# Attention features, Mish layer and top-1 experts on one core: last activation products and logits placed earlier, register loads placed later

## The chip, the cores and the metric

The kernel runs on one core of a Trainium2 chip. The metric is the device time of one execution in microseconds, the median of several runs. The engines are TensorE (PE; its weight loads are listed apart as PEld), VectorE (DVE), ScalarE (ACT), GpSimd (POOL) and SyncE (SP, which here only issues transfers).

## What is computed

Three layers in a row: random-feature attention, a dense layer with Mish as its activation, and a mixture of 8 experts of which each token takes one.

```python
# attention: phi is exp of (projection - norm - max); per head
num = q_p @ (k_p.T @ v);  den = q_p @ sum(k_p) + 1e-6;  x = num / den
# dense layer, 1152 tokens, 512 -> 2048 -> 512
h = x @ w_in
g = h * tanh(log1p(exp(h)))
y = g @ w_out
# experts: logits, softmax, the best expert of a token, its place, capacity
logits = y @ w_gate
out[i] = gate_w[i] * (relu(y[i] @ w1[e]) @ w2[e])      # where the place is under the capacity
```

## The kernel before

Matrix products that need float32 are done as three products of rounded halves (`mm3`, L69 to L74): a tile is split into a rounded high half (`round_hi`, L52, on ScalarE, GpSimd or VectorE) and a remainder (`take_lo`, L62, on VectorE or GpSimd).

**Attention**, up to about 76 us. It goes over 8 pairs of heads. For each pair the transposed keys and queries (`kqf`) are loaded, split (`split`, with the engines named by `halves`, L226) and projected (`pj`); VectorE takes the negated maximum (`nm`, L259), ScalarE forms `e` (L266, L269), and TensorE forms the sums `kvp`, transposes (`qt`) and the quotient's parts (`den`, `num`). The order in which the engines get these instructions isn't fixed by hand. For pair 1 the two pieces of `kqf` (512 and 768 columns) are rounded on ScalarE, and GpSimd takes their remainders.

**The h stage**, to about 182 us, from here on in the order written (`tc.manual_schedule()`). It goes over 16 chunks `j` of 128 hidden units, each with three column blocks `c` of 384 tokens: `h` by `hmm`, the copy to `g` by `hout`, and beside them the conversion of the next weights (`conv64` through `advance(wi)`, `advance(wo1)`: generators that issue one VectorE instruction at each step), the pieces of the activation (`mish`: sigmoid, logarithm, tanh on ScalarE, then the product `tp` on VectorE, L500), and the gate weights. These fold `w_out` into `w_gate`: `wturn(j)` transposes a chunk of `w_out` into `woT` on VectorE (L465), `wgate(b)` multiplies four such chunks (`wu`, L471) after chunks 4, 8 and 12. The logits (`lg`, L506) are then made from `g` itself, four chunks at a time.

**y of group 1**, from about 185 to 218 us. The tokens are in four groups of 288. The loop over 16 chunks multiplies `g` by `w_out` (`ymm`, 12 products a chunk). `g_split(j + 2)` rounds `g` two chunks ahead, in three buffers; `wo_split` splits the `w_out` chunks. Into the same loop are written the last activation products (`mish("tp", ...)`), the last logits behind chunk 7, and the routing: `route0` (maximum and place), `route1` (counts), `gates`, and `route2`, a generator that finds the most used expert of group 1 and the group and expert that come second, and loads these numbers into registers (`eA`, `g1`, `eB`; L762 to L764) of SP, VectorE and, for `g1`, ScalarE. `advance(*[chain] * pace)` takes `pace` steps of it a chunk.

**Group 2 and the experts**, to the end. Group 2's `y` goes like group 1's, with its columns chosen by the register `g1`, while the first expert's weights are loaded by SP (`expert_load`, by `eA`). Then the two experts' layers run, each followed by its output: the copies to `yo` (the last at L932), transposes, weighting by `wA` or `wB`, and the transfer to memory. If any token is left over, a slow general path follows; it isn't taken here.

The loop of group 1, in its middle part before the change:

```python
e = "pool" if j < 6 else "act"
if 0 < j < NJ - 2:
    g_split(j + 2, all0, e, "dve")
if 0 < j < NJ - 6:
    wo_split(j + 6, e, "dve")
if j in (4, 5, 6):
    mish("tp", j + 9)
```

Of the kernel before, what the change touches and what calls it, by code (L numbers as in the profile page):

```python
# [33 lines left out]
def performer_mish_moe(  # L34
# [123 lines left out]
    def advance(*gens):  # L158

        for x in gens:  # L160
            next(x, None)

    def finish(*gens):

        for x in gens:
            for _ in x:
                pass
# [18 lines left out]
    with ExitStack() as c2:  # L186
# [38 lines left out]

        def halves(p):  # L226

            return (("act", "dve"),) * 3 if p == 0 else (("act", "pool"),) * 2 if p == 1 else (("pool", "pool"),) * 5

        def split(p):  # L230
            d = st[p]
# [215 lines left out]
    with tc.manual_schedule():  # L447
# [77 lines left out]
        def wo_split(j, ehi, elo):  # L525
            wo_hi(j, ehi)
            wo_lo(j, elo)
# [13 lines left out]
        def ymm(ps, j):  # L541

            t, w = ghl.pop(j), chunk["wo", j]
            for d in range(KT):
                s = slice(d * 128, d * 128 + 128)
                mm3(ps[d][:, :GT], w[0][:, s], w[1][:, s], t[:, 0, :], t[:, 1, :], j == 0, j == NJ - 1)
# [38 lines left out]
        for j in range(NJ):  # L585
            if j + 4 < NJ:
                fetch("wi", j + 4)
            for i in (j + 2,) if j < 12 else (14, 15) if j == 12 else ():
                fetch("wo", i)
            if j == 6:  # L590
                nc.sync.dma_start(
                    out=out.rearrange("(p t) d -> p (t d)", p=128).rearrange("p (c f) -> p c f", f=128),
                    in_=zero[:, None, :].to_broadcast([128, NT * DM // 128 // 128, 128]),
                )
            if j in (9, 13):
                logits((j - 9) // 4)
            wi = convert("wi", j + 3) if j + 3 < NJ else iter(())
            wo1 = convert("wo", j + 1) if j < 14 else iter(())
            wo2 = convert("wo", 15) if j == 13 else iter(())
            for c in range(3):  # L600
                if (j, c) not in h_early:
                    hout(j, c, hmm(j, c))
                if j == 14 and c == 0:
                    wo_hi(0, "pool")
                    wo_hi(1, "pool")
                if j == 15 and c == 0:
                    wo_hi(2, "pool")
                    for i in range(3):
                        g_hi(i, all0, "pool")
                if c == 0:  # L610
                    advance(wi, wo1, late, wi)
                    late = wi
                    if j == 15:
                        wturn(j)
                if c == 1:
                    if j in (4, 8, 12):
                        gates_of[0] = wgate(j // 4 - 1)
                        next(gates_of[0])
                    advance(wi, wi, wo1, wo2)
                    if j in (5, 9, 13):  # L620
                        advance(gates_of[0])
                if c == 2:
                    advance(wo1, wo2)
                    if j in (4, 8, 12, 5, 9, 13):
                        advance(gates_of[0])
                    if j < 15:
                        wturn(j)
                    advance(wo2)
                for x in at.get(3 * j + c, ()):
                    x()  # L630
                if 3 * j + c in (44, 45, 46):
                    wo_lo(3 * j + c - 44, "dve")
                if j == 15 and c > 0:
                    for i in range(3):
                        if (i > 0) == (c == 2):
                            g_lo(i, all0, "dve")
                if j == 14 and c == 2:
                    fpool.release()
                    y3 = tc.alloc_tile_pool(name="y3", bufs=3, side="right", reuse_waits="tile")
                    whA = tc.alloc_tile_pool(name="whA", bufs=7, side="right", reuse_waits="tile")  # L640
# [89 lines left out]
        def route2():  # L730
# [28 lines left out]
            R["ri"] = ri  # L759
            ET = mybir.EngineType  # L760
            why = "an index computed from constants and a maximum's place"
            R["eA"] = nc.values_load(ri[0:1, 0:1], engines=[ET.SP, ET.DVE], min_val=0, max_val=E - 1, skip_runtime_bounds_check_because=why)  # L762
            R["g1"] = nc.values_load(ri[0:1, 1:2], engines=[ET.SP, ET.DVE, ET.Activation], min_val=0, max_val=G - 2, skip_runtime_bounds_check_because=why)
            R["eB"] = nc.values_load(ri[0:1, 2:3], engines=[ET.SP, ET.DVE], min_val=0, max_val=E - 1, skip_runtime_bounds_check_because=why)  # L764
            wA, wB = small("wA", [TT, 3]), small("wB", [TT, 3])
            V.tensor_copy(out=wA, in_=R["wt"][:, 0:3, ds(R["eA"], 1)].rearrange("p t e -> p (t e)"))
            yield
            V.tensor_copy(out=wB, in_=R["wt"][:, ds(R["g1"] * 3 + 3, 3), ds(R["eB"], 1)].rearrange("p t e -> p (t e)"))
            yield
            R["wA"], R["wB"] = wA, wB  # L770
            rem = small("rem", [1, 1])
# [55 lines left out]
        for j in range(NJ):  # L827

            if j == 0:
                for i in range(3, 7):  # L830
                    wo_lo(i, "dve")
            e = "pool" if j < 6 else "act"
            if 0 < j < NJ - 2:
                g_split(j + 2, all0, e, "dve")
            if 0 < j < NJ - 6:
                wo_split(j + 6, e, "dve")
            if j in (4, 5, 6):
                mish("tp", j + 9)
            advance(*[chain] * pace)
            ymm(ps0, j)  # L840
            if j in (2, 3):
                advance(gates_of[0])
            if j == 7:
                logits(3)
                lgs = h3.tile([128, NT], F32, name="lgs", tag="em2")
                S.copy(out=lgs[:, 0:384], in_=lg[0])
                V.tensor_copy(out=lgs[:, 384:768], in_=lg[1])
                S.copy(out=lgs[:, 768:1152], in_=lg[2])
            if j == 8:
                finish(route0(lgs))  # L850
            if j == 11:
                route1()
            if j == 12:
                chain, pace = route2(), 7
                advance(chain)
            if j == 13:
                finish(gates())
        advance(*[chain] * 40)
        colB = ds(R["g1"] * GT + GT, GT)
        g_split(0, colB, "act", "dve")  # L860
        g_split(1, colB, "act", "dve")
# [4 lines left out]
        for j in range(NJ):  # L866
            if j + 2 < NJ:
                g_split(j + 2, colB, "act", "dve")
            ymm(ps1, j)
            expert_load(R["eA"], 0, j)  # L870
            if j >= 4:
                expert_split(0, j - 4, "act", "dve")
# [56 lines left out]
                (S.copy if d % 2 else V.tensor_copy)(out=yo[:, d, :], in_=py[d][:, :GT])  # L929
        for t in range(3):  # L930
            c = slice(t * TT, t * TT + TT)
            (V.tensor_copy if t == 1 else S.copy)(out=yo[:, 3, c], in_=py[3][:, c])  # L932
        for t in range(3):
            turn(pt[t], yo, t, 3)
        send(3, slice(384, 512))
# [122 lines left out]
```

## Time and profile before

| | us |
|---|---|
| median of 3 runs | 306.43 (306.09 to 306.73) |
| profiled execution, its own time | 306.35 |
| its span in the profile | 304.6 |
| TensorE busy | 294.3 (97%) |
| VectorE busy | 215.8 (71%) |
| ScalarE busy | 186.5 (61%) |
| GpSimd busy | 76.1 (25%) |

The span is the time between the first and the last instruction of the profile; the execution's own time has what lies around it. Busy time on TensorE counts an instruction from its start to a modelled end, and successive ones overlap. Times in the rows below are from the span's start. A bracket at the end of a timeline's line gives how long the engine sat idle before it and what it waited for.

### The profile page before, as it was taken

How to read it: one execution, taken by the hardware profiler on the slowest of the kernel's cores; microseconds unless marked ns; L12 is line 12 of the kernel's file. 1: busy time of each engine (PE TensorE's matmuls, PEld its weight loads, DVE VectorE, ACT ScalarE, POOL GpSimd, SP SyncE). 2: the span in 40 equal slices, each digit the busy share in tenths (PEclk: the TensorE clock that was granted, in tenths of full speed). 3: DMA queues.
4: the chain of work that ended last, by engine and by line, in shares of the span. 5: the costliest groups of instructions: out<-in, count | busy, mean ns of one | idle time of the engine just before them, and what ended most of it. 6: DMA issues, size and time to landing. Idle time of an engine off the chain costs nothing.

```text
span 304.6 us, 5993 instructions
## 1 busy us (share of the span) xinstructions
PE 294.3 (97%) x2276; PEld 268.9 (88%) x2277; DVE 215.8 (71%) x386; ACT 186.5 (61%) x359; POOL 76.1 (25%) x108
## 2 busy tenths in 40 slices
PE   8899999999999999999999999989999999999992
PEld 4798787876999899979997997959999999999991
DVE  3675648884999999997887199976647764536521
ACT  3898685873195787948975889623446554435311
POOL 1889994233021210001022166700000000000000
PEclk9999999999999999999999999999999999999998
DMA  6866811221166579834530000000336518712011
GB/s 214 298 223 204 301 38 52 87 80 44 67 209 208 164 225 338 294 124 140 182 95 0 2 0 2 0 1 2 93 119 171 160 34 266 226 45 80 0 41 44
DMA packets 18369, 37.09 MB, mean 122 GB/s; under 512 B 1568, under 2 KB 7552, under 8 KB 18336
## 3 DMA queue, kind: packets, MB, share of 16 engines
q1 hardware_dynamic: 18192, 36.53, 37.4%
q8 instruction: 19, 0.31, 0.4%
q10 hardware_dynamic: 144, 0.13, 0.1%
q14 instruction: 14, 0.11, 0.1%
HBM read 33.12 MB, written 3.54 MB: 120 GB/s over the span
## 4 chain that ended last, share of the span: by engine, by line
PE 89%; DVE 5%; issue 2%; DMA 2%; ACT 1%; POOL 0%; DVEq 0%; SPq 0%; POOLq 0%
PE h L72 12%; PE h L74 11%; PE h L73 11%; PE py L72 7%; PE py L73 7%; PE py L74 7%; PE kvp L278 4%; PE num L311 3%; PE ph L72 3%; PE pj L72 3%; PE ph L74 3%; PE pj L74 3%; PE ph L73 3%; PE lg L506 3%; PE qt L299 3%; PE pj L73 2%
## 5 line engine op out<-in xcount | busy, mean ns | idle before, releaser
L72 PE MATMUL h<-xh,wih 128*128 128x384 f32 x192 | 65.4, 340 | 0.0
L74 PE MATMUL h<-xh,wil 128*128 128x384 f32 x192 | 64.3, 335 | 0.0
L73 PE MATMUL h<-xl,wih 128*128 128x384 f32 x192 | 64.2, 334 | 0.0
L72 PEld LDWEIGHTS h<-xh,wih 128*128 128x128 f32 x192 | 36.0, 188 | 2.9 <-issue 1.5
L73 PE MATMUL py<-gh,whi 128*128 128x288 f32 x128 | 37.8, 296 | 0.6 <-DVE gh L63 0.5
L72 PE MATMUL py<-gh,whi 128*128 128x288 f32 x128 | 38.2, 299 | 0.0
L63 DVE TENSOR_TENSOR wl<-wl,whi 128x512 fp32r<-128x512 f32 x48 | 34.3, 720 | 5.3 <-PE py L74 3.6
L74 PE MATMUL py<-gh,wl 128*128 128x288 f32 x128 | 37.7, 294 | 0.0
L456 ACT COPY g<-h 128x384 f32<-128x384 f32 x42 | 20.1, 478 | 26.7 <-PE h L74 26.6
L73 PEld LDWEIGHTS h<-xl,wih 128*128 128x128 f32 x192 | 36.1, 188 | 0.0
L74 PEld LDWEIGHTS h<-xh,wil 128*128 128x128 f32 x192 | 36.0, 188 | 0.0
L259 DVE TENSOR_REDUCE nm<-pj 128x4 f32<-128x512 f32 x36 | 24.4, 684 | 13.0 <-PE pj L74 12.9
L58 POOL TENSOR_SCALAR wih<-wif 128x512 fp32r<-128x512 f32 x13 | 12.8, 986 | 78.6 <-PE h L73 47.4
L266 ACT ACTIVATE e<-pj,nm 128x128 f32<-128x128 f32 x72 | 22.8, 379 | 10.3 <-DVE nm L259 6.9
L500 DVE TENSOR_TENSOR g<-g,em 128x1152 f32<-128x1152 f32 x16 | 22.3, 1393 | 8.8 <-ACT em L498 8.8
L72 PEld LDWEIGHTS py<-gh,whi 128*128 128x128 f32 x128 | 24.0, 188 | 1.3 <-POOL whi L58 0.6
L73 PEld LDWEIGHTS py<-gh,whi 128*128 128x128 f32 x128 | 24.1, 188 | 1.1 <-DVE gh L63 1.1
L63 POOL TENSOR_TENSOR kql<-kqf,kqh 128x256 fp32r<-128x256 f32 (+2 forms) x29 | 22.6, 799 | 7.5 <-ACT kqh L56 7.3
L74 PEld LDWEIGHTS py<-gh,wl 128*128 128x128 f32 x128 | 24.1, 188 | 0.0
L63 DVE TENSOR_TENSOR gh<-g,gh 128x288 fp32r<-128x288 f32 x32 | 16.6, 526 | 8.6 <-ACT gh L56 8.2
L56 ACT CAST gh<-g 128x288 fp32r (+1 forms) x24 | 10.4, 432 | 19.2 <-PE py L74 13.8
L72 PE MATMUL pj<-omh,kqh 128*128 128x256 f32 x70 | 21.7, 309 | 0.0
(152 smaller groups left out, 711.0 us busy)
## 6 DMA issues: line engine op xcount, KB each, us to landing
wi<-w_in SPq DMA_DIRECT2D x16, 512.0 KB, 3.4
wo<-w_out SPq DMA_DIRECT2D x16, 512.0 KB, 4.2
wl<-w SPq DMA_DIRECT2D x32, 256.0 KB, 2.9
out<-zero SPq DMA_DIRECT2D x1, 2304.0 KB, 11.8
kqf<-kq SPq DMA_DIRECT2D x3, 640.0 KB, 4.5
v<-va SPq DMA_DIRECT2D x4, 390.0 KB, 4.6
kqf<-kq SPq DMA_DIRECT2D x3, 512.0 KB, 3.9
v<-va SPq DMA_DIRECT2D x4, 260.0 KB, 4.1
```

The costliest lines, as they stand in the source:

```text
L56: S.copy(out=hi, in_=src)
L58: P.tensor_scalar(out=hi, in0=src, scalar1=1.0, scalar2=0.0, op0=ALU.mult, op1=ALU.add)
L63: (P if eng == "pool" else V).tensor_tensor(out=lo, in0=src, in1=hi.bitcast(F32), op=ALU.subtract)
L72: T.matmul(out=o, lhsT=lh, rhs=rh, start=start, stop=False)
L73: T.matmul(out=o, lhsT=lh, rhs=rl, start=False, stop=False)
L74: T.matmul(out=o, lhsT=ll, rhs=rh, start=False, stop=stop)
L259: d["max"] = V.tensor_reduce(out=nm, in_=pv, op=ALU.max, axis=AX.X, negate=True)
L266: S.activation(out=e[:, j, :], in_=pv[:, j, :], func=AF.Exp, bias=nm[:, j : j + 1])
L278: T.matmul(out=K[:, c : c + 65], lhsT=e[t][:, h, :], rhs=v[:, (2 * t + h) * 65 : (2 * t + h + 1) * 65], start=(p % 2 == 0 and h == 0 and t ...
L299: T.transpose(q[:, t * 128 : t * 128 + 128], e[t][:, 2 + h, :], ident)
L456: (S.copy if 2 < j or c == 2 else V.tensor_copy)(out=g(j, slice(c * 384, c * 384 + 384)), in_=ps)
L500: V.tensor_tensor(out=hv, in0=hv, in1=em.pop(j), op=ALU.mult)
```

## The change

- `halves`: the second piece of pair 1 is rounded on VectorE instead of ScalarE.
- h stage: the fourth chunk of a block of `woT` is turned at column block 1 instead of 2, ahead of the other steps of the weight conversions there; the last block's fourth chunk stays where it was.
- Group 1: GpSimd rounds in chunks 0 to 4 instead of 0 to 5. The activation products of 13, 14 and 15 come at chunks 3, 4 and 5, ahead of that chunk's `w_out` split. The splits of `w_out` come at 7 and 8 in chunks 1 and 2, at 9 in chunk 5, and then at `j + 4`. `route1` comes behind chunk 10, `route2` begins behind 11, `gates` behind 12.
- Registers: SP loads `eA` and `eB`, then `g1` goes to SP, VectorE and ScalarE, in chunk 14. VectorE's own loads of `eA` and `eB`, the copies of `wA` and `wB` and the count of left-over tokens follow as steps beside group 2.
- The last copies: all three to `yo` on ScalarE.

```diff
@@ -225,7 +225,7 @@
 
         def halves(p):
 
-            return (("act", "dve"),) * 3 if p == 0 else (("act", "pool"),) * 2 if p == 1 else (("pool", "pool"),) * 5
+            return (("act", "dve"),) * 3 if p == 0 else (("act", "pool"), ("dve", "pool")) if p == 1 else (("pool", "pool"),) * 5
 
         def split(p):
             d = st[p]
@@ -616,14 +616,17 @@
                     if j in (4, 8, 12):
                         gates_of[0] = wgate(j // 4 - 1)
                         next(gates_of[0])
-                    advance(wi, wi, wo1, wo2)
+                    advance(wi)
+                    if j % 4 == 3 and j < 15:
+                        wturn(j)
+                    advance(wi, wo1, wo2)
                     if j in (5, 9, 13):
                         advance(gates_of[0])
                 if c == 2:
                     advance(wo1, wo2)
                     if j in (4, 8, 12, 5, 9, 13):
                         advance(gates_of[0])
-                    if j < 15:
+                    if j % 4 < 3:
                         wturn(j)
                     advance(wo2)
                 for x in at.get(3 * j + c, ()):
@@ -759,13 +762,16 @@
             R["ri"] = ri
             ET = mybir.EngineType
             why = "an index computed from constants and a maximum's place"
-            R["eA"] = nc.values_load(ri[0:1, 0:1], engines=[ET.SP, ET.DVE], min_val=0, max_val=E - 1, skip_runtime_bounds_check_because=why)
+            one = lambda c, eng: nc.values_load(ri[0:1, c : c + 1], engines=[eng], min_val=0, max_val=E - 1, skip_runtime_bounds_check_because=why)
+            R["eA"], R["eB"] = one(0, ET.SP), one(2, ET.SP)
             R["g1"] = nc.values_load(ri[0:1, 1:2], engines=[ET.SP, ET.DVE, ET.Activation], min_val=0, max_val=G - 2, skip_runtime_bounds_check_because=why)
-            R["eB"] = nc.values_load(ri[0:1, 2:3], engines=[ET.SP, ET.DVE], min_val=0, max_val=E - 1, skip_runtime_bounds_check_because=why)
+            yield
+
+            eA, eB = one(0, ET.DVE), one(2, ET.DVE)
             wA, wB = small("wA", [TT, 3]), small("wB", [TT, 3])
-            V.tensor_copy(out=wA, in_=R["wt"][:, 0:3, ds(R["eA"], 1)].rearrange("p t e -> p (t e)"))
-            yield
-            V.tensor_copy(out=wB, in_=R["wt"][:, ds(R["g1"] * 3 + 3, 3), ds(R["eB"], 1)].rearrange("p t e -> p (t e)"))
+            V.tensor_copy(out=wA, in_=R["wt"][:, 0:3, ds(eA, 1)].rearrange("p t e -> p (t e)"))
+            yield
+            V.tensor_copy(out=wB, in_=R["wt"][:, ds(R["g1"] * 3 + 3, 3), ds(eB, 1)].rearrange("p t e -> p (t e)"))
             yield
             R["wA"], R["wB"] = wA, wB
             rem = small("rem", [1, 1])
@@ -829,13 +835,13 @@
             if j == 0:
                 for i in range(3, 7):
                     wo_lo(i, "dve")
-            e = "pool" if j < 6 else "act"
+            e = "pool" if j < 5 else "act"
             if 0 < j < NJ - 2:
                 g_split(j + 2, all0, e, "dve")
-            if 0 < j < NJ - 6:
-                wo_split(j + 6, e, "dve")
-            if j in (4, 5, 6):
-                mish("tp", j + 9)
+            if j in (3, 4, 5):
+                mish("tp", j + 10)
+            for i in {1: (7,), 2: (8,), 5: (9,)}.get(j, (j + 4,) if 5 < j < NJ - 4 else ()):
+                wo_split(i, e, "dve")
             advance(*[chain] * pace)
             ymm(ps0, j)
             if j in (2, 3):
@@ -848,14 +854,18 @@
                 S.copy(out=lgs[:, 768:1152], in_=lg[2])
             if j == 8:
                 finish(route0(lgs))
+            if j == 10:
+                route1()
             if j == 11:
-                route1()
+                chain, pace = route2(), 4
+                advance(chain)
             if j == 12:
-                chain, pace = route2(), 7
-                advance(chain)
-            if j == 13:
                 finish(gates())
-        advance(*[chain] * 40)
+                pace = 3
+            if j > 12:
+                pace = 14 - j if j < 15 else 0
+        while "g1" not in R:
+            next(chain)
         colB = ds(R["g1"] * GT + GT, GT)
         g_split(0, colB, "act", "dve")
         g_split(1, colB, "act", "dve")
@@ -867,6 +877,8 @@
             if j + 2 < NJ:
                 g_split(j + 2, colB, "act", "dve")
             ymm(ps1, j)
+            if j > 0:
+                advance(chain)
             expert_load(R["eA"], 0, j)
             if j >= 4:
                 expert_split(0, j - 4, "act", "dve")
@@ -929,7 +941,7 @@
                 (S.copy if d % 2 else V.tensor_copy)(out=yo[:, d, :], in_=py[d][:, :GT])
         for t in range(3):
             c = slice(t * TT, t * TT + TT)
-            (V.tensor_copy if t == 1 else S.copy)(out=yo[:, 3, c], in_=py[3][:, c])
+            S.copy(out=yo[:, 3, c], in_=py[3][:, c])
         for t in range(3):
             turn(pt[t], yo, t, 3)
         send(3, slice(384, 512))
```

## Rows read from the trace of the kernel before

**Rows 1.** Windows: us; busy us (count) of PE, PEld, DVE, ACT, POOL; clock, DMA, GB/s.

```profile
182.00:220.00 38.00, 36.01 (x316) 31.32 (x315) 30.60 (x72) 20.29 (x32) 10.91 (x13) 1.00 0.05 13
...
226.00:250.00 24.00, 24.00 (x183) 24.00 (x182) 16.38 (x30) 13.61 (x31) 0.00 (x0) 1.00 0.42 121
```

**Rows 2.** Waits of TensorE: who waited for whom, us in total, times, longest.

```profile
PE lg L506 <- DVE g L500: 1.4, 1, 1.4
...
PE wu L471 <- PE h L74: 0.6, 1, 0.6
```

**Rows 3.** Timeline of VectorE at the first gate weights: start us, us, engine, line, operation.

```profile
99.82 0.68 DVE L127 SCALAR_TENSOR_TENSOR wl<-wo,wl 128x512 int32<-128x512 int32 x1
...
101.44 0.70 DVE L465 STREAM_TRANSPOSE woT<-wl 128x512 f32<-128x512 f32 x1
```

**Rows 4.** Timeline of TensorE around logits in the h stage: start us, us.

```profile
131.89 0.34 PE L74 MATMUL h<-xh,wil 128*128 128x384 f32 x1
...
134.23 0.44 PE L72 MATMUL h<-xh,wih 128*128 128x384 f32 x1
```

**Rows 5.** Timeline of TensorE in group 1 and at the start of group 2.

```profile
196.99 0.29 PE L72 MATMUL py<-gh,whi 128*128 128x288 f32 x1
...
197.66 0.29 PE L74 MATMUL py<-gh,wl 128*128 128x288 f32 x1
...
198.85 0.29 PE L74 MATMUL py<-gh,wl 128*128 128x288 f32 x1
...
203.58 0.40 PE L72 MATMUL py<-gh,whi 128*128 128x288 f32 x1
...
218.47 0.29 PE L72 MATMUL py<-gh,whi 128*128 128x288 f32 x1
...
219.46 0.29 PE L74 MATMUL py<-gh,wl 128*128 128x288 f32 x1
```

**Rows 6.** Timeline of VectorE in group 1.

```profile
192.01 0.86 DVE L63 TENSOR_TENSOR gh<-g,gh 128x288 fp32r<-128x288 f32 x1
...
196.92 0.44 DVE L63 TENSOR_TENSOR gh<-g,gh 128x288 fp32r<-128x288 f32 x1
...
197.89 1.34 DVE L500 TENSOR_TENSOR g<-g,em 128x1152 f32<-128x1152 f32 x1
...
217.84 0.17 DVE L766 COPY wA<-wt 96x3 f32 x1 [1.31 <-issue]
```

**Rows 7.** Timeline of ScalarE in group 1: the last three tanh.

```profile
190.45 3.28 ACT L498 ACTIVATE em<-em 128x1152 f32<-128x1152 f32 x3
```

**Rows 8.** Timeline of all engines at the end: the last copies.

```profile
298.24 0.24 ACT L932 COPY yo<-py 128x96 f32<-128x96 f32 x1 [2.14 <-PE py L74]
298.51 0.26 DVE L932 COPY yo<-py 128x96 f32<-128x96 f32 x1 [2.28 <-ACT yo L932]
...
298.80 0.24 ACT L932 COPY yo<-py 128x96 f32<-128x96 f32 x1 [0.33 <-DVE yo L932]
```

**Rows 9.** Timeline of all engines at the start.

```profile
7.34 1.88 DVE L259 TENSOR_REDUCE nm<-pj 128x4 f32<-128x512 f32 x3
...
7.92 1.27 POOL L63 TENSOR_TENSOR kql<-kqf,kqh 128x512 fp32r<-128x512 f32 x1 [6.49 <-ACT kqh L56]
...
8.05 0.63 ACT L266 ACTIVATE e<-pj,nm 128x128 f32<-128x128 f32 x2 [0.22 <-DVE nm L259]
...
9.07 0.85 ACT L56 CAST kqh<-kqf 128x768 fp32r<-128x768 f32 x1
...
9.79 1.17 ACT L266 ACTIVATE e<-pj,nm 128x128 f32<-128x128 f32 x4
...
10.24 0.30 PEld L278 LDWEIGHTS kvp<-v,e 128*128 128x128 f32 x2 [0.22 <-ACT e L266]
...
11.90 0.19 PEld L74 LDWEIGHTS pj<-omh,kql 128*128 128x128 f32 x1 [0.20 <-POOL kql L63]
```

**Rows 10.** Timeline of TensorE's weight loads in the attention stage: one such wait.

```profile
39.90 0.19 PEld L72 LDWEIGHTS pj<-omh,kqh 128*128 128x128 f32 x1 [0.47 <-issue]
```

## The prediction

> **What bounds the kernel now.** I read the windows first: they say which engine limits each stage. In group 1's stretch (182 to 220 us) TensorE is busy 36.01 of 38.00 us and VectorE 30.60; from 226 to 250 us TensorE is busy throughout, with VectorE at 16.38 of 24 [rows 1]. So a gap on TensorE in group 1 is time lost, and behind it stands a stage that passes an earlier start on one for one. TensorE's list of waits then names the gaps: the logits wait 1.4 us for VectorE's last activation products (`g`, L500), and the gate weights' product (`wu`) waits 0.6 us [rows 2]. TensorE's timeline gives the whole loss of a gap, from the last product before it to the next behind it. Undisturbed logits, in the h stage, take 134.23 - 131.89 = 2.34 us from the h product before to the one behind [rows 4]; those of group 1 take 203.58 - 198.85 = 4.73 us [rows 5]. Two smaller gaps are in the same timeline, both with products that usually start 0.13 us apart: chunk 7's second product, waiting for the low half of its g, lies in 196.99 to 197.66; the first chunk of group 2 waits likewise in 218.47 to 219.46 [rows 5].
>
> **The change, part by part.** The sums are made on the profiled execution (306.35 us, span 304.6), which is 0.08 us under the median 306.43; the savings are taken from the median.
>
> *Logits at chunk 7.* Now VectorE does the three activation products at chunks 4, 5 and 6 and rounding remainders of w_out between them. The change puts them at 3, 4 and 5 and moves the w_out splits of 9 and on behind them. I lay VectorE's new order out with its own durations. The remainder of g for chunk 5 starts at 192.01 as now [rows 6], since everything ahead of it stands as before. It takes 0.44 us where GpSimd is idle, an activation product 1.34 [rows 6]. So: chunk 5 done at 192.45, product 13 at 193.79, chunk 6 at 194.23, product 14 at 195.57, chunk 7 at 196.01, product 15 at 197.35. ScalarE's tanh for the three is over at 190.45 + 3.28 = 193.73, the first of them near 191.5 [rows 7], so no product waits for it. TensorE asks for chunk 7's remainder at 196.99 + 0.13 = 197.1, for the logits at 199 [rows 5]: both come in time, by 1.1 and 1.6 us. Saved: 4.73 - 2.34 = **2.39 us** at the logits and 0.67 - 0.26 = **0.41 us** at chunk 7. ScalarE takes over GpSimd's rounding from chunk 5 on: g of chunk 7 behind its tanh at 193.73, and it has 17.7 us free in the stretch [rows 1]. The displaced w_out splits each come four chunks ahead of their use, over 6 us. Nothing there issues a DMA.
>
> *Routing and the hand-over.* The routing moves up one chunk; it is as many instructions, all behind work that TensorE has in hand. VectorE's three register loads now stop it for 1.31 us before the copy of wA [rows 6], and the remainders for group 2's first two chunks stand behind that, which is TensorE's gap of 0.99 - 0.26 = **0.73 us** [rows 5]. After the change VectorE loads one register at chunk 14, a third of 1.31 or 0.44 us, and both remainders can be done while TensorE is in chunks 14 and 15, over 3 us. The other two loads and the copies go beside group 2, where VectorE has 7.6 of 24 us free and works two chunks ahead [rows 1]; I cost them at nothing, and without that cover they would cost their 0.9 us. On SP the same three loads stand ahead of the same expert transfers, in another order and earlier; on ScalarE the load of g1 has chunk 14 to hide in. Saved: 0.73 us.
>
> *woT.* The fourth transpose of a block now starts at 101.44 and takes 0.70 us [rows 3]; TensorE's 0.6 us before `wu` [rows 2] are a wait for it (the list names the h product, but that is long issued, and the transpose ends at 102.14). Placed ahead of the w_out conversions that now begin at 99.82 [rows 3] it is done 1.6 us sooner. Those end when the transpose ends now, and their tile is used a chunk later. The h stage is TensorE's own throughout, so the **0.6 us** stays. For the later blocks no such wait is listed: nothing there.
>
> *The last copies.* The three copies to `yo` alternate ScalarE, VectorE, ScalarE, each starting after the other engine's: 298.24, 298.51, 298.80, the last over at 299.04 [rows 8]. On one queue they need no hand-over; at 0.24 us each without overlap they would end at 298.96 (0.08 saved), and with the overlap of successive ScalarE instructions (two take 0.63 and four 1.17, so 0.27 for each further one against 0.36 for the first) near 298.78 [rows 8, 9]. VectorE's own first weighting, 0.35 us behind the first transpose, then limits. I take **0.2 us**.
>
> *The start.* One cast of 128x768 moves from ScalarE (0.85 us) to VectorE [rows 9]. Nothing shows it on VectorE; by the maxima there, three in 1.88 us for 512 columns each [rows 9], it would be 0.94, and I take ScalarE's 0.85. A gain is bounded by TensorE's two waits nearby, for ScalarE's e at 10.24 (0.22) and GpSimd's kql at 11.90 (0.20): 0.42 us [rows 9]. A loss is worked out below: 0.6. As TensorE has projections to go on with meanwhile, I take **0**, between the ends.
>
> Sum: 2.39 + 0.41 + 0.73 + 0.6 + 0.2 = 4.33 us, that is 306.43 - 4.33 = **302.1 us**.
>
> **The rivals.**
>
> *The cast is held by GpSimd.* VectorE and GpSimd lengthen each other: g's remainder takes 0.86 us beside GpSimd's rounding and 0.44 without [rows 6]. At the start GpSimd works on kql from 7.92 for 1.27 us, until 9.19, and VectorE's first maximum ends near 8.0 [rows 9]. If the cast waits there, it ends near 10.0, the second maximum near 10.6, and e behind it, now at 9.79 [rows 9], starts near 10.65. VectorE is then 0.9 late; ScalarE, which has lost its 0.85 us cast, catches up a part, and I put 0.6 on the end: **302.7 us**. For it: the 0.86. Against: TensorE's projections cover.
>
> The Trainium skill ("SBUF — State Buffer", section Who interferes with whom) has such a rule: VectorE in a two-port mode and GpSimd hold a shared pair of ports exclusively, and the second to start blocks until the first is done. The trace's 0.86 against 0.44 agrees with it in kind [rows 6]; by it this rival is the case.
>
> *The cast is free.* TensorE gets the whole 0.42 us: **301.7 us**.
>
> *VectorE is late all the same.* If every step from 192.01 on went at its long value (0.86 for a remainder, and with the same 0.42 more 1.76 for a product [rows 6]), chunk 7's remainder would be done at 192.01 + 3 x 0.86 + 2 x 1.76 = 198.1, 1.0 us after TensorE asks; product 15, at 199.9, would still meet the delayed logits. **303.1 us**. Against: GpSimd's last rounding there is chunk 6's, so at most one or two steps are long.
>
> *The hand-over keeps its gap*, because another engine's register comes as late: 0.73 less, **302.8 us**.
>
> *The attention stage gets another order, and slower.* It lies outside the manual schedule, and its instructions don't run in the order written, so an edit there can shuffle all of it, to 76 us. What a poor order costs is a weight load that waits 0.47 us after a 32-column step [rows 10]; twelve such rows stand between 30 and 76 us. Nine more would eat the gain (306.3, no change); ten leave 306.8, and from there on it is slower: at eleven **307.3 us**. Against: one cast of 0.85 us moved hardly doubles the gaps of the stage.
>
> **How the numbers follow.** A measurement of this kernel tells 0.2%, 0.6 us, from no change. Chances: the forecast 0.50, the cast held 0.14, the cast free 0.12, VectorE late 0.12, the hand-over kept 0.06, another order 0.06, half of it no change and half slower. So faster 0.94, same 0.03, slower 0.03. The range reaches down to the free cast, and 0.4 further, as each of the four gaps is read from starts and good to some 0.1: 301.3. It reaches up past VectorE late to the held cast together with the kept hand-over, 303.4.
>
> **What would show it.** Right: the waits list no longer has `lg` behind L500; from the last product of chunk 7 to the first of chunk 8 TensorE takes 2.3 to 2.4 us; group 2 starts without the 0.99 us step; `wu` follows the h product at once; three copies of `yo` stand on ScalarE in a row. The attention stage should end as now, give or take 0.5 us. Wrong would be a new wait for g or wl at chunks 5 to 8, VectorE's products later than 198, an attention stage over a microsecond longer, or a wait in group 2 behind VectorE's register loads.

## The result, and the profile after the change

The changed kernel takes 302.50 us (median of 4 runs, 302.18 to 302.58) against 306.31 us (306.09 to 306.73) of the kernel before: a ratio of 0.9872 [0.9855, 0.9889], 3.81 us faster. Forecast were 302.1 us in a range of 301.3 to 303.4. The profiled execution took 302.44 us with a span of 300.7; before it was 306.35 with 304.6. So the spans differ by 3.91 us.

The head of the page gives the busy time of the engines, then the chain of waits that ended last.

```profile
PE 292.8 (97%) x2276; PEld 269.5 (90%) x2277; DVE 214.6 (71%) x386; ACT 187.9 (62%) x363; POOL 75.2 (25%) x104
...
PE 95%; DMA 1%; DVE 1%; SPq 0%; ACT 0%; issue 0%
```

Busy time has hardly moved (TensorE 294.3 before, VectorE 215.8). No work went away; gaps did. TensorE now has 95% of the chain, where it had 89%, and VectorE's share fell from 5 to 1%.

TensorE's list of waits, which named the gaps before, is now this:

```profile
PE wp L200 <- DVE wb L197: 1.2, 1, 1.2
PE qt L299 <- DVE e L264: 0.4, 1, 0.4
PE pt L821 <- ACT yo L944: 0.3, 1, 0.3
```

That is all of it. Both rows of [rows 2] are missing, the logits' and the one before `wu`. The windows of group 1 and group 2, with the columns of [rows 1], show the same from the other side:

```profile
178.00:215.00 37.00, 37.00 (x329) 33.56 (x328) 31.62 (x70) 24.21 (x39) 10.07 (x12) 1.00 0.03 11
222.00:246.00 24.00, 24.00 (x183) 24.00 (x182) 16.62 (x33) 13.52 (x30) 0.00 (x0) 1.00 0.40 121
```

In group 1 TensorE was busy 36.01 of 38 us and is now busy throughout. (The new window begins some 6 us ahead of group 1, so the other columns don't compare one by one.) TensorE's timeline answers to [rows 4, 5] (start us, us):

```profile
196.03 0.30 PE L72 MATMUL py<-gh,whi 128*128 128x288 f32 x1
196.16 0.30 PE L73 MATMUL py<-gh,whi 128*128 128x288 f32 x1
196.30 0.29 PE L74 MATMUL py<-gh,wl 128*128 128x288 f32 x1
...
197.48 0.29 PE L74 MATMUL py<-gh,wl 128*128 128x288 f32 x1
197.71 2.14 PE L506 MATMUL lg<-g,wg 128*32 128x384 f32 x24
199.78 0.40 PE L72 MATMUL py<-gh,whi 128*128 128x288 f32 x1
...
214.66 0.30 PE L72 MATMUL py<-gh,whi 128*128 128x288 f32 x1
214.80 0.30 PE L73 MATMUL py<-gh,whi 128*128 128x288 f32 x1
214.93 0.30 PE L74 MATMUL py<-gh,wl 128*128 128x288 f32 x1
```

Read three distances in it, from start to start. From the product before the logits to the one behind, 199.78 - 197.48 = 2.30 us, where the undisturbed ones of [rows 4] take 2.34. In chunk 7, from the first product to the third, 0.27 us instead of 0.67. In the first chunk of group 2, 0.27 instead of 0.99.

Why VectorE is in time now is in its own timeline, which answers to [rows 6]:

```profile
191.05 0.45 DVE L63 TENSOR_TENSOR gh<-g,gh 128x288 fp32r<-128x288 f32 x1
191.42 1.34 DVE L500 TENSOR_TENSOR g<-g,em 128x1152 f32<-128x1152 f32 x1
192.69 0.18 DVE L481 COPY wg<-ws 128x32 f32<-128x32 f32 x1
193.09 0.46 DVE L63 TENSOR_TENSOR gh<-g,gh 128x288 fp32r<-128x288 f32 x1 [0.23 <-POOL gh L58]
193.47 1.35 DVE L500 TENSOR_TENSOR g<-g,em 128x1152 f32<-128x1152 f32 x1
194.74 0.45 DVE L63 TENSOR_TENSOR gh<-g,gh 128x288 fp32r<-128x288 f32 x1
195.10 1.35 DVE L500 TENSOR_TENSOR g<-g,em 128x1152 f32<-128x1152 f32 x1
196.37 0.68 DVE L63 TENSOR_TENSOR wl<-wl,whi 128x512 fp32r<-128x512 f32 x1
...
217.84 0.17 DVE L772 COPY wA<-wt 96x3 f32 x1 [0.46 <-DVE gh L63]
```

It is the order that the prediction laid out, at the short durations (0.45 and 1.35 us), with two things that the prediction left out: the copy to `wg` (0.18) and a wait of 0.23 us for GpSimd's rounding of chunk 6. Chunk 7's remainder ends at 195.19, 0.97 us before TensorE's second product of that chunk; the last activation product ends at 196.45, 1.26 us before the logits. The copy of `wA` no longer follows 1.31 us of register loads in front of group 2.

The whole difference, stage by stage. The boundaries are starts of TensorE's weight loads; the last two rows are bounded by the end of the last weighting and the end of the span:

| stage | before | after | saved | forecast |
|---|---|---|---|---|
| start to the last `num` | 75.33 | 75.02 | 0.31 | 0 |
| last `num` to the first `wu` | 26.88 | 26.26 | 0.62 | 0.6 |
| first `wu` to the first product of group 1 | 83.22 | 83.19 | 0.03 | 0 |
| to the first load of the last logits | 13.65 | 13.24 | 0.41 | 0.41 |
| to the next `y` product | 4.50 | 2.07 | 2.43 | 2.39 |
| to the first expert product | 40.86 | 40.28 | 0.58 | 0.73 |
| to the last `py` | 53.33 | 53.39 | -0.06 | 0 |
| to the end of the last weighting | 2.02 | 1.75 | 0.27 | 0.2 |
| to the end of the span | 4.80 | 5.49 | -0.69 | 0 |

The rows between the start and the closing stage save 4.28 us, where 4.33 were forecast. Two rows are not in the sum at all, the first and the last. Whether the change makes them is for the experiments to tell.

### The profile page after: what moved, and what is told of

Its sections match the earlier page's. It is cut to its first block, busy times and chain, and to the rows that moved or that the text cites. A ratio compares the mean times of both kernels' runs of the same rounds, so it can differ in the third digit from the quotient of the medians.

```text
span 300.7 us, 5990 instructions
## 1 busy us (share of the span) xinstructions
PE 292.8 (97%) x2276; PEld 269.5 (90%) x2277; DVE 214.6 (71%) x386; ACT 187.9 (62%) x363; POOL 75.2 (25%) x104
## 4 chain that ended last, share of the span: by engine, by line
PE 95%; DMA 1%; DVE 1%; SPq 0%; ACT 0%; issue 0%
PE h L72 12%; PE h L74 11%; PE h L73 11%; PE py L72 9%; PE py L74 8%; PE py L73 8%; PE kvp L278 5%; PE num L311 3%; PE ph L72 3%; PE ph L74 3%; PE ph L73 3%; PE pj L72 3%; PE pj L74 3%; PE lg L506 3%; PE qt L299 3%; PE pj L73 2%
## 5 line engine op out<-in xcount | busy, mean ns | idle before, releaser
L58 POOL TENSOR_SCALAR wih<-wif 128x512 fp32r<-128x512 f32 x13 | 14.6, 1126 | 76.1 <-PE h L73 39.8
L56 ACT CAST whi<-wl 128x512 fp32r<-128x512 f32 x39 | 23.1, 616 | 0.0
```

Source lines behind the costliest of these rows:

```text
L56: S.copy(out=hi, in_=src)
L58: P.tensor_scalar(out=hi, in0=src, scalar1=1.0, scalar2=0.0, op0=ALU.mult, op1=ALU.add)
```

## The experiments

Each of the twelve kernels was timed against the kernel before on the same chip. The medians of two variants differ by less than their intervals in most cases, so the verdicts are read from the traces, and the medians only have to agree.

| run | median, us | ratio to the kernel before |
|---|---|---|
| again | 302.14 | 0.9865 [0.9846, 0.9885] |
| undo_start | 301.75 | 0.9846 [0.9829, 0.9863] |
| undo_tail | 302.21 | 0.9867 [0.9845, 0.9890] |
| undo_regs | 302.29 | 0.9855 [0.9834, 0.9876] |
| split_first | 303.31 | 0.9887 [0.9848, 0.9926] |
| tp_late | 302.14 | 0.9853 [0.9816, 0.9889] |
| pool6 | 302.67 | 0.9878 [0.9839, 0.9916] |
| undo_woT | 302.75 | 0.9869 [0.9832, 0.9906] |
| route_late | 302.48 | 0.9868 [0.9845, 0.9890] |
| logits_only | 303.10 | 0.9894 [0.9878, 0.9911] |
| free_cast | 302.70 | 0.9873 [0.9851, 0.9894] |
| start_only | 306.50 | 0.9994 [0.9982, 1.0006] |

### The changed kernel once more

No edit: the changed kernel is profiled and timed a second time, to see which rows of the table hold.

> The changed kernel once more, nothing edited, as the yardstick of this call. Open: from the end of the last weighting to the end of the span the changed kernel's profile has 5.49 us (295.20 to 300.69), the kernel before 4.80 (299.80 to 304.60). If that is chance of one execution, this profile shows anything from 4.7 to 5.5 and the median stays at 302.5; if it belongs to the change, it is 5.4 to 5.6 again. The attention stage (first h products, den and num done) ended 0.31 us earlier than before, with the first keys landing 0.55 us earlier; if that landing is chance, this profile can differ by as much.

Measured: 302.14 us, 4.47 below the 306.61 of the kernel before beside it. The stages in the middle came out as in the first profile, but the two rows that the forecast had left at nothing moved: the last `num` at 74.50 instead of 75.02, and from the last weighting to the span's end 4.85 us instead of 5.49. Both differ by half a microsecond and more between executions of one and the same kernel, so neither can be put down to the change from one pair of profiles.

### The start: the cast back on ScalarE, alone, and without GpSimd

Three runs ask what the edit of `halves` is worth. The first undoes it in the changed kernel, the second makes it alone in the kernel before.

```diff
-return (("act", "dve"),) * 3 if p == 0 else (("act", "pool"), ("dve", "pool")) if p == 1 else (("pool", "pool"),) * 5
+return (("act", "dve"),) * 3 if p == 0 else (("act", "pool"),) * 2 if p == 1 else (("pool", "pool"),) * 5
```

> The changed kernel with the second piece of pair 1 rounded on ScalarE again. Theory (the cast on VectorE is held by GpSimd: it took 1.31 us, 7.99 to 9.30, while GpSimd was on kql until 8.87): undone, the second maximum comes earlier, and the time stays within 0.2 us or falls by up to 0.4. Rival (ScalarE's 0.85 us was what the stage waited for): undone, the attention stage ends 0.3 to 0.4 us later and the time rises by as much.

> The kernel before with the cast of pair 1's second piece on VectorE alone. Theory (the edit is worth nothing, the 0.31 us that the attention stage ended earlier came with the first keys' earlier landing): the time within 0.4 us of the kernel before's; its attention stage ends at 75.0 to 75.4 if the second landing is near 6.5 us and near 74.5 if it is near 5.7. Rival (the edit itself gives 0.3): it ends 0.3 earlier than 75.33 even with the late landing.

The third takes the cover away that the prediction's first rival needs: pair 1's first remainder goes to VectorE, so that GpSimd is idle when VectorE casts.

```diff
-return (("act", "dve"),) * 3 if p == 0 else (("act", "pool"), ("dve", "pool")) if p == 1 else (("pool", "pool"),) * 5
+return (("act", "dve"),) * 3 if p == 0 else (("act", "dve"), ("dve", "pool")) if p == 1 else (("pool", "pool"),) * 5
```

> The changed kernel with pair 1's first remainder on VectorE too, so that GpSimd has nothing to do when VectorE's cast of 768 columns runs. Theory (GpSimd holds the cast): it takes 0.4 to 0.9 us, where it took 1.08 to 1.49 in the executions in which GpSimd was at work on kql as it started, and 0.73 where GpSimd was nearly through. Rival (the cast is that long by itself): 1.1 us or more again. The attention stage: VectorE has 0.7 us more, so its end is within 0.5 us of the changed kernel's, whichever way.

The cast, and GpSimd's remainder, in the timeline of all engines of the changed kernel; then VectorE's timeline of the run with the edit alone and of the one without GpSimd:

```profile
7.58 1.29 POOL L63 TENSOR_TENSOR kql<-kqf,kqh 128x512 fp32r<-128x512 f32 x1 [6.15 <-ACT kqh L56]
...
7.99 1.31 DVE L60 CAST kqh<-kqf 128x768 fp32r<-128x768 f32 x1
```

```profile
8.52 1.44 DVE L60 CAST kqh<-kqf 128x768 fp32r<-128x768 f32 x1 [0.63 <-DMA kqf<-kq]
```

```profile
8.21 0.56 DVE L60 CAST kqh<-kqf 128x768 fp32r<-128x768 f32 x1
```

Free, the cast takes 0.56 us; beside GpSimd's remainder it took 1.02 to 1.49 in nine profiles, and 0.73 in a tenth, where it began near that remainder's end. So the rival's mechanism is true: VectorE's cast is held. In the changed kernel it ends 9.30 - 8.87 = 0.43 us behind GpSimd's remainder, and in all ten 0.41 to 0.43 behind it, wherever it began. The 0.86 against 0.44 us that the prediction gave for this rival are those of an instruction with two inputs; that a cast, which has one, is held is shown only here. The Trainium skill ("SBUF — State Buffer", section Who interferes with whom) has an instruction of VectorE in a two-port mode and one of GpSimd shut each other out, so that the second to start is blocked until the first is done. The traces agree nearly: blocked in full, the cast would still have its 0.56 us to go, and it has 0.41 to 0.43. But the rival's price, 0.6 us, was not paid. What the stage's end follows is ScalarE's cast of pair 1's first piece, and that waits for its transfer, as ScalarE's timeline of the changed kernel shows (first profile, then the second):

```profile
6.88 0.62 ACT L56 CAST kqh<-kqf 128x512 fp32r<-128x512 f32 x1 [0.47 <-DMA kqf<-kq]
```

```profile
6.36 0.62 ACT L56 CAST kqh<-kqf 128x512 fp32r<-128x512 f32 x1 [0.27 <-DMA kqf<-kq]
```

The two starts are 0.52 us apart, and so are the last `num` (75.02 and 74.50). The distance from the start of this cast to the last `num` is nearly the same in all profiles but one: 68.11 us in the three without the edit (before, undo_start, logits_only) and 68.10 to 68.16 in the ten with it, over starts from 6.36 to 7.58. The edit is worth nothing, to 0.05 us, in either direction, and the 0.31 us of the first comparison is the landing of a transfer, the moment at which its data have arrived. (The exception is free_cast, 68.54: VectorE there has a remainder of 0.68 us more to do at that point, which would fit.) (The end in start_only, 75.67, lies later than was expected for it; its cast of the first piece began at 7.57.) The times agree: 306.50 with the edit alone, no change, and 301.75 without it, not told apart from 302.14.

### The order at the logits

One run puts the `w_out` splits ahead of the activation products again, one keeps the new order but a chunk later, one gives GpSimd its sixth chunk back.

```diff
 g_split(j + 2, all0, e, "dve")
+if 0 < j < NJ - 6:
+    wo_split(j + 6, e, "dve")
 if j in (3, 4, 5):
     mish("tp", j + 10)
-for i in {1: (7,), 2: (8,), 5: (9,)}.get(j, (j + 4,) if 5 < j < NJ - 4 else ()):
-    wo_split(i, e, "dve")
```

> The changed kernel with the w_out splits of 9, 10 and 11 back ahead of the activation products at chunks 3, 4 and 5 (GpSimd and VectorE together, as before), the products' chunks unchanged. Theory (what closed the logits' wait is that the splits moved behind the products, as VectorE has no room for both): product 15 ends 1.4 us later, near 198.7 where the logits want it at 198.1 by the changed kernel's times, and chunk 7's remainder is 0.7 late; together 0.5 to 0.9 us lost between the first product of group 1 and the first behind the logits. Rival (the products' earlier chunk alone closed it): no loss, within 0.1 us.

```diff
-if j in (3, 4, 5):
-    mish("tp", j + 10)
+if j in (4, 5, 6):
+    mish("tp", j + 9)
```

> The changed kernel with the activation products at chunks 4, 5 and 6 again, one chunk later, the splits behind them as changed. Theory (order against the splits): product 15 ends near 197.6, in time for the logits: no loss, within 0.1 us from group 1's first product to the first behind the logits. Rival (their chunk): the logits wait again, 0.4 us or more lost there.

```diff
-e = "pool" if j < 5 else "act"
+e = "pool" if j < 6 else "act"
```

> The changed kernel with GpSimd rounding in chunk 5 too (g of chunk 7 and w_out 9), as before. Theory (GpSimd's share decides nothing, there is room): VectorE's remainder of chunk 7 comes up to 0.8 us later, wanted 1.1 us after it was done; no loss, within 0.1 us. Rival (VectorE and GpSimd hold each other up, so GpSimd must be out of the way): chunk 7 or the logits wait, 0.2 to 0.6 us lost there.

From the first product of group 1 to the product behind the logits the kernel before takes 18.15 us and the changed one 15.31. With the chunk put back (tp_late) and with GpSimd's share put back (pool6) it stays at 15.31; with the splits ahead it is 16.65, a loss of 1.34 us, more than the 0.5 to 0.9 expected. TensorE's waits of split_first, and then VectorE's timeline there:

```profile
PE py L73 <- DVE gh L63: 0.6, 2, 0.4
```

```profile
192.53 0.91 DVE L63 TENSOR_TENSOR wl<-wl,whi 128x512 fp32r<-128x512 f32 x1
193.35 1.76 DVE L500 TENSOR_TENSOR g<-g,em 128x1152 f32<-128x1152 f32 x1
...
195.14 0.44 DVE L63 TENSOR_TENSOR gh<-g,gh 128x288 fp32r<-128x288 f32 x1
195.50 0.68 DVE L63 TENSOR_TENSOR wl<-wl,whi 128x512 fp32r<-128x512 f32 x1
196.11 1.34 DVE L500 TENSOR_TENSOR g<-g,em 128x1152 f32<-128x1152 f32 x1
197.38 0.45 DVE L63 TENSOR_TENSOR gh<-g,gh 128x288 fp32r<-128x288 f32 x1
```

Each product stands behind a split, and the first is stretched to 1.76 us beside GpSimd's rounding (192.86 to 193.91 us). The remainders of chunks 6 and 7 start at 195.14 and 197.38, when TensorE has begun these chunks (195.13 and 197.22) and wants them 0.13 us later. From the first product of a chunk to the third TensorE takes 0.74 us in chunk 6 and 0.89 in chunk 7 instead of 0.27, and it loses another 0.18 at the logits.

So with the splits behind the products neither the earlier chunk nor GpSimd's smaller share is needed. They aren't without effect, though: with the splits ahead, the two together still bring 18.15 down to 16.65, that is 1.50 of the 2.84 us. The order with both of them put back was not run. And split_first undoes two things, for the splits from 9 on go back ahead of the products and two chunks earlier as well. In pool6 the stretched steps are there (0.86 for a remainder, 1.58 for a product), and still in time.

### woT turned at its old place

```diff
-advance(wi)
-if j % 4 == 3 and j < 15:
-    wturn(j)
-advance(wi, wo1, wo2)
+advance(wi, wi, wo1, wo2)
...
-if j % 4 < 3:
+if j < 15:
     wturn(j)
```

> The changed kernel with the fourth transpose of a block back at the third column block. Theory: TensorE waits 0.6 us before the first gate weights' product again, the stretch from the last num to that product is 26.9 instead of 26.3 us, and it stays lost: the time rises by 0.6. Rival (a wait is taken back later in the h stage, where something else limits): the wait returns but group 1 starts less than 0.2 us later.

From the last `num` to the first `wu` it took 26.88 us, as before the change, and the wait is back in TensorE's list:

```profile
PE wu L471 <- PE h L74: 0.6, 1, 0.6
```

The last block of `wu` begins 80.25 us after the first, in the changed kernel 80.24: nothing of the 0.6 us is made up in the h stage. In the changed kernel the transpose stands where the prediction put it, ahead of the conversion. Counted from the last `num` it ends 1.61 us sooner than before, at 100.22, and so 1.06 us before `wu` begins; VectorE's timeline, then TensorE's:

```profile
99.52 0.70 DVE L465 STREAM_TRANSPOSE woT<-wl 128x512 f32<-128x512 f32 x1
100.15 0.79 DVE L127 SCALAR_TENSOR_TENSOR wl<-wo,wl 128x512 int32<-128x512 int32 x1
```

```profile
101.02 0.34 PE L74 MATMUL h<-xh,wil 128*128 128x384 f32 x1
101.28 1.08 PE L471 MATMUL wu<-woT,wgf 128*32 128x128 f32 x32
```

### The hand-over: fewer loads, or an earlier place

The change does two things at once where group 1 hands over to group 2. One run gives VectorE all three registers and the copies ahead of group 2 again, but leaves the routing a chunk earlier; the other puts the routing back to its old chunks, but keeps the single load.

```diff
-one = lambda c, eng: nc.values_load(ri[0:1, c : c + 1], engines=[eng], min_val=0, max_val=E - 1, skip_runtime_bounds_check_because=why)
-R["eA"], R["eB"] = one(0, ET.SP), one(2, ET.SP)
+one = lambda c, eng: nc.values_load(ri[0:1, c : c + 1], engines=[ET.SP, ET.DVE], min_val=0, max_val=E - 1, skip_runtime_bounds_check_because=why)
+R["eA"] = one(0, None)
...
-yield
-eA, eB = one(0, ET.DVE), one(2, ET.DVE)
+R["eB"] = one(2, None)
...
-while "g1" not in R:
-    next(chain)
+advance(*[chain] * 40)
...
-if j > 0:
-    advance(chain)
```

> The changed kernel with VectorE loading all three registers in chunk 14 and doing the copies of wA, wB and the count of left-over tokens ahead of group 2, as before; the routing stays one chunk earlier. Theory of the prediction (the three loads instead of one make the gap): a wait of 0.3 to 0.7 us for the first low half of group 2 returns. Rival (the routing's place alone closed it: ready 211.4, three loads of 0.43 and copies of 1.0 end at 213.8, first low half at 214.2, wanted at 214.5): no wait, time within 0.1 us.

```diff
-if j == 10:
-    route1()
 if j == 11:
-    chain, pace = route2(), 4
-    advance(chain)
+    route1()
 if j == 12:
+    chain, pace = route2(), 7
+    advance(chain)
+if j == 13:
     finish(gates())
-    pace = 3
-if j > 12:
-    pace = 14 - j if j < 15 else 0
+    pace = 1
+if j == 14:
+    pace = 0
```

> The changed kernel with the routing back at its old chunks (counts behind 11, the generator behind 12, gates behind 13); VectorE still loads one register ahead of group 2 and the rest beside it. From the count's product to the first product of the expert's layer the changed kernel has 32.01 us, or 30.43 without the one chunk that the routing stands earlier; the kernel before 31.00. Theory after the first call (place or fewer loads, each alone closes the gap): here fewer loads leave g1 ready near 213.5, ScalarE's first rounding done at 214.15 and the remainder at 214.65, wanted at 214.53 by the changed kernel's times, so 0.1 to 0.2 us of wait: 30.5 to 30.7. Rival (only the place does it): 30.9 to 31.0, as before.

With the three loads back VectorE stops again, for 1.46 us, but beside chunk 14, as the timeline of undo_regs shows:

```profile
213.00 0.17 DVE L770 COPY wA<-wt 96x3 f32 x1 [1.46 <-issue]
```

TensorE sees nothing of it: 40.28 us from the product behind the logits to the first expert product, as in the changed kernel, and the expected wait of 0.3 to 0.7 us for a remainder doesn't come. With the old chunks and one load TensorE doesn't wait either, not even the 0.1 to 0.2 us expected: it takes 40.10 us, and both remainders are done by 214.34, before group 2 begins at 214.81, as VectorE's timeline of route_late shows:

```profile
213.39 0.95 DVE L63 TENSOR_TENSOR gh<-g,gh 128x288 fp32r<-128x288 f32 x2 [0.51 <-ACT gh L56]
```

Either half of the edit closes the gap. The three loads cost time only where they are made at the old place, right in front of group 2's remainders, as in the kernel before.

### The logits alone

The kernel before with the order of the products and splits and GpSimd's share, and with nothing else of the change.

```diff
-e = "pool" if j < 6 else "act"
+e = "pool" if j < 5 else "act"
...
-if 0 < j < NJ - 6:
-    wo_split(j + 6, e, "dve")
-if j in (4, 5, 6):
-    mish("tp", j + 9)
+if j in (3, 4, 5):
+    mish("tp", j + 10)
+for i in {1: (7,), 2: (8,), 5: (9,)}.get(j, (j + 4,) if 5 < j < NJ - 4 else ()):
+    wo_split(i, e, "dve")
```

> The kernel before with the order of the activation products, the w_out splits and GpSimd's share alone. Theory (the parts add): from group 1's first product to the first behind the logits 15.31 us as in the changed kernel, 18.15 before, so 2.84 saved; the count's product to the expert's layer 31.0 as before, the gate weights' wait of 0.6 still there; the time near 306.4 - 2.8 = 303.6. Rival (the earlier logits are partly lost at the hand-over, where the routing now has less time): the hand-over costs 0.3 or more beyond its 31.0.

303.10 us. The 15.31 us are reached without the other edits, 40.84 us to the experts stay as before, and TensorE's list keeps the two gaps of the other edits:

```profile
PE wu L471 <- PE h L74: 0.6, 1, 0.6
PE py L73 <- DVE gh L63: 0.5, 1, 0.5
```

The parts add up, then. The time was half a microsecond under the expectation; in the profile the landing was early (this cast at 6.64, last `num` at 74.75) and the closing stage short (4.85 us).

### The last copies

```diff
-S.copy(out=yo[:, 3, c], in_=py[3][:, c])
+(V.tensor_copy if t == 1 else S.copy)(out=yo[:, 3, c], in_=py[3][:, c])
```

> The changed kernel with the middle copy of the last three to yo on VectorE again. Theory (hand-overs between engines): the last weighting ends 0.28 us later after the last product than in the changed kernel, and the time rises by 0.2 to 0.3. Rival (the closing transfer takes back what comes early, 0.7 us longer after the change): the span from the last weighting's end shrinks by as much, and the time stays within 0.1.

All engines at the end, of the changed kernel and then of undo_tail:

```profile
293.92 0.52 ACT L944 COPY yo<-py 128x96 f32<-128x96 f32 x3 [2.13 <-PE py L74]
...
294.57 0.63 DVE L827 TENSOR_SCALAR o<-pt,wB 96x128 f32<-96x128 f32 x2 [2.64 <-PE pt L821]
```

```profile
293.45 0.24 ACT L944 COPY yo<-py 128x96 f32<-128x96 f32 x1 [2.13 <-PE py L74]
293.72 0.26 DVE L944 COPY yo<-py 128x96 f32<-128x96 f32 x1 [2.27 <-ACT yo L944]
...
294.01 0.24 ACT L944 COPY yo<-py 128x96 f32<-128x96 f32 x1 [0.32 <-DVE yo L944]
```

Three copies on one engine take 0.52 us in all; alternating they take 0.80. From the last `py` to the end of the weighting it is 1.74 or 1.75 us in the two profiles of the changed kernel and 2.02 here: 0.28 us, as before the change. The timing (302.21 against 302.14) doesn't resolve so little.

### The closing stage

No run was made for it, but all show it. From the last weighting to the span's end it took 4.77 to 5.49 us over the 14 profiles: 4.80, 5.37 and 4.85 in those whose end is as before the change (the kernel before, start_only, logits_only), 5.49 and 4.85 in the two of the changed kernel, 5.43 with the copies undone. The edits don't sort it. What stands in it are SyncE's waits, here of the kernel before and of the changed one:

```profile
SPq L949 <- SPq L949: 2.0, 2, 1.6
```

```profile
SPq L961 <- SPq L961: 2.7, 2, 2.3
```

The longest grew from 1.6 to 2.3 us, the 0.69 us of the table. It comes behind the issue of the last transfer to memory and ends with that transfer's landing. The profile's rows of this transfer, with its time from issue to landing at the end, are these for the kernel before, the changed kernel and the changed kernel once more:

```profile
out<-o SPq DMA_DIRECT2D x1, 144.0 KB, 3.0
```

```profile
out<-o SPq DMA_DIRECT2D x1, 144.0 KB, 3.7
```

```profile
out<-o SPq DMA_DIRECT2D x1, 144.0 KB, 3.1
```

Over the 14 profiles it takes 2.97 to 3.69 us, and what is left of the closing stage is 1.79 or 1.80 us in each. So the stage is as long as this landing makes it. Why the same 144 KB land later in one execution than in another stays open.

## Why the prediction was right

*Logits at chunk 7: right, and for the reason given.* 2.39 and 0.41 us were forecast, 2.43 and 0.41 came. The margins were a little smaller than laid out, 0.97 and 1.26 us instead of 1.1 and 1.6, by the copy to `wg` and GpSimd's wait. The rival "VectorE is late all the same" didn't come: in no run is every step long, as its 1.0 us supposes. VectorE was late in split_first, and there in another way, by two more splits (0.91 and 0.68 us) ahead of chunk 7's remainder.

*woT: right.* 0.6 forecast, 0.62 measured, and the run that undoes it loses just that.

*The hand-over: right in the gap, off in its reason and a little in its size.* The gap itself went entirely, 0.99 to 0.27 us. The prediction put that on fewer loads, "a third of 1.31 or 0.44 us", together with the place; the runs show that each alone is enough. The load itself is mis-sized: the one in chunk 14 took 0.55 us in the trace, like the first of the three before the change, and the second and third 0.31 each. Of the 0.73 us, 0.58 are left at the experts: in group 2's first six chunks TensorE's products are 0.1333 us apart now, where they were 0.1311 behind the stall, some 0.03 us a chunk. Over the 14 profiles this follows the place of the routing: 0.1333 in the ten that have it a chunk earlier, undo_regs with its three loads among them, and 0.1311 in the four that have it at the old chunks. One of these is route_late, which has no stall, and there the saving is 40.86 - 40.10 = 0.76. So the earlier routing costs 0.18 us that fewer loads alone would have kept; how it acts on the distance is open. The rival that the gap stays didn't come.

*The last copies: right in kind, mis-sized by 0.07.* 0.2 was taken, between 0.08 without overlap and 0.26 with it; it was 0.27, so the copies do overlap on one engine.

*The start: right at 0, between two rivals that both had something.* The cast is held, as the first says, and it is free of cost, though not by the second's gain: the 0.42 us of waits nearby were not on the path, as the last `num` follows the landing of `kqf`. The third, another order of the stage, didn't come: its end moves with the landing alone.

*What the sum left out: the closing stage.* The sum was 4.33 us and the spans differ by 3.91. Of the difference 0.69 is lost behind the last weighting and 0.31 won at the start, both with the landing of a transfer, by chance of the execution; the rest is the 0.15 of the hand-over against 0.10 gained in the other rows. The two timings of the change, 3.81 and 4.47 us, lie on either side of the sum. The range held the result, but it had no term for either end of the program, where executions of one kernel differ by half a microsecond.

*A faster version* was not found: undo_start has the lowest median, 301.75, but its interval overlaps that of the changed kernel, and its trace gives no reason for a gain. The trace of route_late is 0.18 us shorter up to the experts, which is too little to be seen in its median, 302.48.

## What to carry to other kernels

Where one engine serves several deadlines in order, lay its queue out with the measured durations and put what has slack (here splits used four chunks later) behind what has a deadline. With the splits out of the way the products' chunk mattered nothing; with the splits back ahead 1.34 us were lost. VectorE's 1.46 us of register loads were free where they stood further ahead of the need than they lasted, and there a shorter stop gained nothing. Before a difference of half a microsecond at the start or the end of a program is credited to an edit, take the same kernel's profile twice and find the event that the stage follows; here it is the landing of a transfer at both ends.

## What was not expected of the hardware

- A cast of 128x768 took 0.56 us on VectorE alone and 1.02 to 1.49 beside GpSimd's remainder of pair 1's first piece (nine profiles; 0.73 in a tenth, near that remainder's end), ending 0.41 to 0.43 us behind it, and cost the kernel nothing.
- The attention stage's end kept its distance from one cast that waits for a transfer to 0.06 us (68.10 to 68.16) over landings that differed by 1.2 us.
- Products of 288 columns, each with its weight load, come 0.1311 or 0.1333 us apart in the same stretch of group 2, by the place of the routing in group 1, at a granted clock of 1.00.
- Behind the last weighting, 4.77 to 5.49 us pass to the end of the span, whatever the edit: 2.97 to 3.69 from the issue of the last transfer to its landing, and 1.79 or 1.80 besides.
- A register load took VectorE 0.55 us right behind the instruction that wrote the number, and 0.30 to 0.32 otherwise.
